# VectorE's program for a unit of experts: one text per class of size, odd and even together, weight pieces behind tests

## The chip, the cores and the metric

The kernel runs on one core of a Trainium2 chip. The metric is device time of one execution in microseconds; the time before is 594.67 us, the median of three runs (593.29 to 596.66). TensorE multiplies, ScalarE and VectorE work on tiles, GpSimd (POOL) gathers and scatters rows, and SyncE (SP) issues most DMAs. Each engine runs its own program and waits for the others on semaphores.

## The reference, cut to what matters

Attention over keys and values pooled by 8, then a mixture of 8 experts that sends each of the 4608 rows to one expert (top 1).

```python
k_p = k.reshape(B, H, Sp, 8, D).mean(axis=3)         # v likewise; B, H, S, D = 8, 8, 576, 64
attn = softmax(scale * q @ k_p.T); x = (attn @ v_p)  # -> x: 4608 rows of 512
expert_idx = np.argmax(x @ w_gate, axis=1)           # 8 experts
gate_w = softmax(x @ w_gate)[row, expert_idx]
for e in range(8):
    h = np.maximum(x[expert_idx == e] @ w1[e], 0.0)  # 512 -> 1024
    out[expert_idx == e] = gate_w * (h @ w2[e])      # 1024 -> 512
```

## The kernel before

**Stages.** The first 190 us or so are attention and routing: every row gets its expert and is scattered to a buffer in DRAM, sorted by expert. The rest is the expert stage, which the change concerns. There each expert's rows are cut into *units* of up to 512 rows (four blocks of 128). A unit's size is counted in halves of 64 rows, n from 1 to 8. How many units there are and how large is known only at run time: the kernel computes a table, every engine loads a unit's entries into registers and takes branches on them. The program text has 16 units one after the other, of which those above the number found are left out by a branch. With the inputs used there are 13, of sizes 8, 8, 1, 6, 4, 8, 5, 8, 4, 1, 8, 8, 6 (units 0 to 12); units 2, 3, 4, 5, 7, 9 and 10 open a new expert, so new weights come with them.

**One unit.** X (512 columns by rows) is split into a high and a low part for matmuls in fp32r; so are the weights W (eight pieces a expert, 0 to 3 of the first matrix, 4 to 7 of the second) and the hidden tiles H (eight, f = 0 to 7). ScalarE writes the high parts, VectorE the low ones: the high part is read back and subtracted (`hlo`, `hlo1` for H, `xlo` for X, `wlo` for W). TensorE multiplies X by W into H's banks, three of them in turn (`mm1`, its matmuls are line 890 in the trace): group f is 12 matmuls where n is above 2, and may start when the low part of the tile three before it, which used the same bank, is done; so a unit's fourth group waits for its first H part. Then it multiplies H by the second matrix (line 947) and VectorE scales the result by the gate into Y, block by block from the last; GpSimd scatters Y to the output.

**VectorE in a unit** (`dve_unit`), in the order of the text: (1) H's low parts (`hidden_lo`), with the low parts of weight pieces 4 to 7 between them where the unit is a new expert's, and behind H's sixth tile two transposes of the next unit's first two blocks (`xturn`); (2) the next unit's X (`following`, `next_part`, `xpart`): low parts of blocks 0 and 1, transposes of blocks 2 and 3, the last block of Y of the running unit (`early`), low parts of blocks 2 and 3, and among them weight pieces 0 to 3 if the next unit opens an expert; (3) two table loads and the rest of Y. An odd n takes three instructions for a Y block of one half, and two instead of one for each H tile.

**What sets the order.** It is written out by hand. A branch picks a text: `hidden_lo` has a text for n = 1, one for n = 2, one for even and one for odd n above 2 (lines 1238 and 1240); `following` has again a text for each of n = 1, above 2 and 2 (lines 1338 and 1343), and `next_part` in each of them one without and one with new weights (line 1268). A jump past a text is a branch of VectorE's own sequencer, which the profile does not count as busy.

## Time and profile before

| | |
|---|---|
| median of three runs | 594.67 us |
| profiled execution, whole | 594.27 us |
| its span, first to last instruction | 592.8 us |
| TensorE busy | 562.5 us (95%) |
| VectorE busy | 374.1 us (63%) |
| ScalarE busy | 241.2 us (41%) |
| GpSimd busy | 197.0 us (33%) |
| mean granted TensorE clock | 0.999 |

The span is the profiled execution's; 1.5 us of the run lie around it. A row of the timeline has the start, the duration (of all instructions merged in it), engine, line, operation, tiles out and in, the count, and in brackets the idle time of that engine before it with what ended it. "issue" there means that the engine waited for nothing that the profile shows. The names of banks in the trace are those of the attention stage, which the expert stage uses again: pP and pq are H's banks, pU is Y's, pS and pm are X's.

### The profile page before, as it was taken

The page shows a single profiled execution, that of the slowest core. Times are in us where ns is not written, and L with a number is a line of the kernel's source. Part 1 is how long each engine was busy: PE and PEld are TensorE (multiplying, and loading weights), DVE is VectorE, ACT ScalarE, POOL GpSimd, SP SyncE. Part 2 cuts the span into 40 slices and gives each one's busy share as a digit, 9 for nine tenths or more (in the row PEclk, how much of TensorE's full clock was granted, in tenths as well). Part 3 has the DMA queues.
Part 4 walks back from the last instruction along what each step waited for, and adds up shares of the span by engine and source line. Part 5 has one row for each costly group of instructions (what it writes and reads, how often), then busy time and mean ns, then how long its engine had stood idle before and what let it go on. Part 6 is the DMA issues. An engine that isn't in the chain of part 4 may idle for free.

```text
span 592.8 us, 13401 instructions
## 1 busy us (share of the span) xinstructions
PE 562.5 (95%) x4334; PEld 499.4 (84%) x4334; DVE 374.1 (63%) x738; ACT 241.2 (41%) x445; POOL 197.0 (33%) x294
## 2 busy tenths in 40 slices
PE   6889999999998999999997999989999999999995
PEld 5778989888887888879996888878899888888994
DVE  6699898888884224567968671684527967244221
ACT  2667686787631102355444420424115742021110
POOL 7456675655251032136222211122022442201101
PEclk9999999999999999999999999999999999999999
DMA  8979999896432647446995852027520860100101
GB/s 312 365 233 283 284 293 297 216 256 173 127 126 73 184 133 258 149 124 215 252 312 160 247 155 80 21 81 214 125 93 20 234 201 23 56 0 35 43 4 56
DMA packets 89019, 96.55 MB, mean 163 GB/s; under 512 B 38174, under 2 KB 69918, under 8 KB 88864
## 3 DMA queue, kind: packets, MB, share of 16 engines
q1 hardware_dynamic: 79472, 74.22, 43.5%
q0 software_dynamic: 8848, 20.55, 9.7%
q8 instruction: 60, 0.98, 0.8%
q14 instruction: 95, 0.78, 0.4%
q10 hardware_dynamic: 544, 0.02, 0.1%
HBM read 72.68 MB, written 26.00 MB: 166 GB/s over the span
## 4 chain that ended last, share of the span: by engine, by line
PE 69%; DVE 10%; issue 6%; POOL 5%; DMA 4%; ACT 3%; DVEq 1%; POOLq 1%; SPq 0%; ACTq 0%
PE pU L947 30%; PE pP L890 18%; PE pq L890 9%; PE pU L323 3%; POOL dispatched L432 2%; DMA XE<-in_v_dram 2%; PE pP L489 2%; DMA w<-in_moe_w_dram 2%; PE pP L307 1%; DVE mx L291 1%; PE pS L287 1%; POOL raw L196 1%; DVE sd L294 1%; DVE raw L196 1%; PE pq L489 1%
## 5 line engine op out<-in xcount | busy, mean ns | idle before, releaser
L947 PE MATMUL pU<-W,H 128*128 128x512 f32 x912 | 200.6, 380 | 4.0 <-DVE Y L1328 1.7
L947 PEld LDWEIGHTS pU<-W,H 128*128 128x128 f32 x912 | 171.5, 189 | 30.1 <-issue 2.5
L890 PE MATMUL pP<-X,W 128*128 128x512 f32 (+3 forms) x660 | 121.9, 340 | 5.8 <-DVE X L1157 3.6
L1545 POOL DMA_INDIRECT out_dram<-Y,GT x51 | 57.8, 1133 | 203.6 <-DVE Y L1330 168.7
L890 PEld LDWEIGHTS pP<-X,W 128*128 128x128 f32 x660 | 108.5, 190 | 15.8 <-DVE X L1157 4.0
L1082 ACT ACTIVATE H<-pP 128x512 fp32r<-128x512 f32 x56 | 33.5, 598 | 140.6 <-PE pP L890 134.2
L1330 DVE TENSOR_SCALAR Y<-pU,GT 128x512 f32<-128x512 f32 x36 | 26.6, 747 | 82.7 <-PE pU L947 81.7
L1103 DVE SCALAR_TENSOR_TENSOR H<-pP,H 128x512 fp32r<-128x512 f32 (+1 forms) x62 | 40.0, 645 | 53.5 <-ACT H L1082 51.4
L1183 ACT CAST W<-ST 128x1024 fp32r<-128x1024 f32 x56 | 56.8, 1051 | 27.5 <-PE pU L947 20.0
L1191 DVE TENSOR_TENSOR W<-ST,W 128x1024 fp32r<-128x1024 f32 x54 | 64.4, 1217 | 1.9 <-ACT W L1183 1.8
L890 PE MATMUL pq<-X,W 128*128 128x512 f32 (+3 forms) x324 | 62.5, 343 | 0.3 <-issue 0.3
L323 PE MATMUL pU<-V,pt 110*128 110x146 f32 (+3 forms) x468 | 56.7, 283 | 2.5 <-ACT pt L308 1.9
L890 PEld LDWEIGHTS pq<-X,W 128*128 128x128 f32 x324 | 53.7, 190 | 5.6 <-issue 0.8
L323 PEld LDWEIGHTS pU<-V,pt 110*128 110x128 f32 (+3 forms) x468 | 51.4, 179 | 4.2 <-ACT pt L308 2.9
L1552 POOL DMA_DIRECT2D GT<-dispatched x44 | 24.3, 552 | 82.9 <-issue 81.6
L432 POOL DMA_INDIRECT dispatched<-xe,ix x36 | 38.9, 1079 | 17.7 <-POOL ix L393 9.8
L1082 ACT ACTIVATE H<-pq 128x512 fp32r<-128x512 f32 x28 | 16.7, 597 | 60.8 <-PE pq L890 60.8
L1152 DVE STREAM_TRANSPOSE pS<-XE 128x512 f32<-128x512 f32 x26 | 37.9, 1499 | 0.0
L308 ACT COPY pt<-pP 110x384 f32<-110x384 f32 x72 | 30.8, 480 | 6.5 <-PE pP L307 5.8
L1103 DVE SCALAR_TENSOR_TENSOR H<-pq,H 128x512 fp32r<-128x512 f32 (+1 forms) x30 | 19.6, 655 | 21.2 <-ACT H L1082 20.6
L1143 ACT CAST X<-pS 128x512 fp32r<-128x512 f32 x34 | 19.2, 588 | 32.9 <-DVE pS L1152 22.6
L300 ACT ACTIVATE P<-sd 128x576 f32<-128x576 f32 x36 | 24.8, 689 | 19.0 <-DVE sd L294 17.1
(208 smaller groups left out, 651.8 us busy)
## 6 DMA issues: line engine op xcount, KB each, us to landing
ST<-in_moe_w_dram SPq DMA_DIRECT2D x56, 512.0 KB, 6.0
raw<-in_k_dram SPq DMA_DIRECT2D x12, 768.0 KB, 8.0
raw<-in_v_dram SPq DMA_DIRECT2D x11, 768.0 KB, 12.3
XE<-dispatched SPq DMA_DIRECT2D x104, 64.0 KB, 3.5
qa<-in_q_dram SPq DMA_DIRECT2D x24, 256.0 KB, 7.6
w<-in_moe_w_dram SPq DMA_DIRECT2D x8, 512.0 KB, 4.5
XE<-dispatched SPq DMA_DIRECT2D x15, 256.0 KB, 4.2
qa<-in_q_dram SPq DMA_DIRECT2D x2, 1024.0 KB, 11.3
```

Of the source, the lines that this page charges most:

```text
L308: take(out=pt[t][a][0:R], in_=pPs[a][0:R, 0 : 3 * P])
L323: nc.tensor.matmul(pu[p0 : p0 + n, a, h * VW : (h + m) * VW], lhsT=pt[t][a][0:r, c % 3 * P + p0 : c % 3 * P + p0 + n], rhs=Vs[g % 2][0:r, ...
L432: apart(nc.gpsimd.indirect_dma_start(out=xs, out_offset=bass.IndirectOffsetOnAxis(ap=at, axis=0), in_=rows, in_offset=None))
L890: r = pe.matmul(out=pH[g % 3][:, :m], lhsT=w1s(w, f, k), rhs=x, start=i == 0, stop=i == len(passes) - 1)
L947: r = pe.matmul(out=pY[:, s % 2, :], lhsT=h, rhs=in_turn(w[:, k * 512 : (k + 1) * 512]), start=start and i == 0, stop=stop and i == len(ps ...
L1082: act.activation(out=HH[:, f, o], in_=src[:, o], func=AF.Relu).then_inc(Q["A_h"], 1)
L1103: return dve.scalar_tensor_tensor(out=dst[:, f, to], in0=src[:, at], scalar=0.0, in1=f32(HH[:, f, at]), op0=ALU.max, op1=ALU.subtract)
L1152: dve.transpose(out=pX[:, s % 2, :].rearrange("p (c a g t) -> p c g t a", c=4, a=2, g=4), in_=XE[u % 2][:, s, :].rearrange("p (g r c) -> p ...
L1183: act.copy(out=(W1H if i < 4 else W2H)[:, o], in_=ST[:, i, :]).then_inc(Q["A_s1" if i < 4 else "A_s2"], 1)
L1191: eng.tensor_tensor(out=(W1L if i < 4 else W2L)[:, o], in0=ST[:, i, :], in1=f32((W1H if i < 4 else W2H)[:, o]), op=ALU.subtract).then_inc( ...
L1330: r = dve.tensor_scalar(out=rows(Y[:, s, :]), in0=a, scalar1=gate, scalar2=None, op0=ALU.mult)
L1545: pool.indirect_dma_start(out=out, out_offset=bass.IndirectOffsetOnAxis(ap=GT[:, u, s, 1:2].bitcast(I32), axis=0), in_=Y[:, s, :], in_offs ...
```

## The change

VectorE's program alone changes; the other engines' instructions stand in the same order. A unit's program is now chosen once by its class of size, n = 1, above 2, or 2, and each class has (1) and (2) in one text (`whole`). Odd and even n above 2 share one text, in which every H tile tests the parity (line 1109). The next unit's X has one text (`next_lo`), with tests around the weight pieces; of these, piece 1 now stands behind the X low parts of blocks 2 and 3 where it stood ahead of them. The order of the classes in the text is n = 1, above 2, 2; behind them stands (3) as before.

```diff
-            r = part(HL, o, o)
-            if odd is not None:
+            if odd is None:
+                part(HL, o, o).then_inc(Q["V_h"], 1)
+                return
+            with dve.If(odd == 0):
+                part(HL, o, o).then_inc(Q["V_h"], 1)
+            with dve.Else():
+                part(HL, o, o)
                 dve.drain()
-                r = part(HH, ds(odd + 64, 64), ds(odd, 64))
-            r.then_inc(Q["V_h"], 1)
+                at = 64 * nc.s_assert_within(entry(dve, K_U, u, 1, 8), 1, 7, ...) - 64
+                part(HH, ds(at + 64, 64), ds(at, 64)).then_inc(Q["V_h"], 1)
...
-        def hidden_lo(u, fs=range(8), small=True):
...
-                with dve.If(n % 2 == 0):
-                    go(8)
-                with dve.Else():
-                    go(7, 64 * ...)
...
+        def hidden_lo(u, n, fs=range(8)):
+            if n > 2:
+                odd = dve.snap(entry(dve, K_U, u, 1, 8) % 2, min_val=0, max_val=1)
+                turns = (lambda: more(dve, u + 1, lambda: [xturn(u + 1, s) for s in range(2)])) if u > 0 else lambda: None
+                return hidden(dve, u, lambda f: hlo(u, f, n, odd), wlo, lambda: vnop("V_s2", 4), fs, False, turns)
+            if n == 2:
+                return hidden(dve, u, lambda f: hlo(u, f, n), wlo, lambda: vnop("V_s2", 4), fs, True)
...
+        def next_lo(u, n, turn, mid=lambda: None):
+            new = entry(dve, K_SW, u, 0, 1) == 1
+            def pieces():
+                mid()
+                if n > 2:
+                    with dve.If(new):
+                        wlo(u, 0)
+            xpart(dve, u, lambda *a: xlo(*a, n <= 2), lambda v: xnone(u, v), pieces, turn)
+            with dve.If(new):
+                for i in range(1 if n != 2 else 0, 4):
+                    wlo(u, i, dve if n == 1 and i == 1 else None)
+            with dve.Else():
+                vnop("V_s1", 4)
...
-            def following():
-                go = lambda turn=None, small=False, **mid: next_part(dve, u + 1, ..., turn, between=0 if small else 2, **mid)
...
-            if u > 0:
-                hidden_lo(u)
-            more(dve, u + 1, following, alone)
+            def whole(size):
+                if size == 1:
+                    hidden_lo(u, 1)
+                    hlo1(u, 1)
+                    more(dve, u + 1, lambda: next_lo(u + 1, 1, None))
+                    return early()
+                hidden_lo(u, size)
+                more(dve, u + 1, lambda: next_lo(u + 1, size, early if size > 2 else None), early if size > 2 else lambda: None)
+                if size == 2:
+                    early()
+
+            if u == 0:
+                next_lo(1, 8, None, early)
+            else:
+                with dve.If(n < 2):
+                    whole(1)
+                with dve.Else():
+                    with dve.If(n > 2):
+                        whole(8)
+                    with dve.Else():
+                        whole(2)
```

**VectorE from unit 4's last H part to unit 5's weight pieces.** Line numbers after the change are five higher for X's parts and W's. Before, as it stands in the text for even n with new weights:

```order
L1103 SCALAR_TENSOR_TENSOR H<-pP_65,H 128x512
L1238 UNCONDITIONAL_BRANCH
...
L1338 COMPARE_AND_BRANCH
...
L1343 COMPARE_AND_BRANCH
L1268 COMPARE_AND_BRANCH
...
L1157 TENSOR_TENSOR X<-pS,X 128x8x64 x2
...
L1191 TENSOR_TENSOR W<-ST,W 128x1024 x2
L1132 COMPARE_AND_BRANCH
L1157 TENSOR_TENSOR X<-pS,X 128x8x64
```

and now:

```order
L1109 COMPARE_AND_BRANCH
L1103 SCALAR_TENSOR_TENSOR H<-pP_65,H 128x512
L1109 UNCONDITIONAL_BRANCH
...
L1162 TENSOR_TENSOR X<-pS,X 128x8x64 x2
L1124 COMPARE_AND_BRANCH
...
L1264 COMPARE_AND_BRANCH
L1196 TENSOR_TENSOR W<-ST,W 128x1024
L1264 UNCONDITIONAL_BRANCH
L1137 COMPARE_AND_BRANCH
L1162 TENSOR_TENSOR X<-pS,X 128x8x64
```

Before, the first dots leave out 75 rows, the second 53, the third 44, all jumped over; now only the odd variant's four rows lie between H and X, and one piece instead of two stands ahead of the second X parts.

**VectorE at the end of the one-half program of unit 2**, from the last weight pieces to the table loads that stand ahead of Y's last blocks. Before:

```order
L1191 TENSOR_TENSOR W<-ST,W 128x1024 x3
L1271 UNCONDITIONAL_BRANCH
L1358 COMPARE_AND_BRANCH
...
L824 COPY scr<-scr 128x1
L1370 UNCONDITIONAL_BRANCH
...
L771 TENSOR_LOAD tab
```

and now:

```order
L1196 TENSOR_TENSOR W<-ST,W 128x1024 x3
L1268 UNCONDITIONAL_BRANCH
...
L1342 COMPARE_AND_BRANCH
...
L824 COPY scr<-scr 128x1
L1354 UNCONDITIONAL_BRANCH
...
L771 TENSOR_LOAD tab
```

The instructions are the same, but from the last jump to the table load it is 148 rows of the text before and 198 now, since the hidden tiles of the two other classes stand behind this program where they stood ahead of it. At the end of the last unit, before the change, the jump past everything that belongs to a next unit is 198 rows long too.

## Rows read from the trace of the kernel before

**Rows 1.** The page: busy time by engine, and one instruction queue (packets, MB, share).
```profile
PE 562.5 (95%) x4334; PEld 499.4 (84%) x4334; DVE 374.1 (63%) x738; ACT 241.2 (41%) x445; POOL 197.0 (33%) x294
...
q14 instruction: 95, 0.78, 0.4%
```

**Rows 2.** TensorE's waits from 200 us on: us, times, longest; seven rows.
```profile
PE pP L890 <- DVE X L1157: 3.6, 1, 3.6
PE pU L947 <- DVE Y L1328: 1.7, 1, 1.7
...
PE pU L947 <- DVE H L1103: 0.8, 1, 0.8
...
PE pU L947 <- DVE W L1191: 0.2, 1, 0.2
```

**Rows 3.** Timeline of TensorE, unit 5's start: start, us, what, [idle before].
```profile
326.61 2.86 PE L890 MATMUL pP<-X,W 128*128 128x512 f32 x12 [3.64 <-DVE X L1157]
```

**Rows 4.** Timeline of VectorE, unit 4's end and unit 5's X.
```profile
316.04 0.68 DVE L1103 SCALAR_TENSOR_TENSOR H<-pP,H 128x512 fp32r<-128x512 f32 x1
318.95 1.29 DVE L1157 TENSOR_TENSOR X<-pS,X 128x512 fp32r<-128x512 f32 x2 [2.23 <-issue]
320.15 2.92 DVE L1152 STREAM_TRANSPOSE pS<-XE 128x512 f32<-128x512 f32 x2
...
323.03 2.33 DVE L1191 TENSOR_TENSOR W<-ST,W 128x1024 fp32r<-128x1024 f32 x2
325.28 1.28 DVE L1157 TENSOR_TENSOR X<-pS,X 128x512 fp32r<-128x512 f32 x2
```

**Rows 5.** Timeline of ScalarE, X's high part of block 1.
```profile
314.45 0.59 ACT L1143 CAST X<-pS 128x512 fp32r<-128x512 f32 x1 [0.83 <-DVE pS L1152]
```

**Rows 6.** Timeline of VectorE, unit 6's end and unit 7's X.
```profile
385.18 0.22 DVE L1103 SCALAR_TENSOR_TENSOR H<-pP,H  x1 [0.21 <-issue]
386.70 1.29 DVE L1157 TENSOR_TENSOR X<-pS,X 128x512 fp32r<-128x512 f32 x2 [1.29 <-issue]
```

**Rows 7.** Timeline of VectorE, first X part behind units 5 and 8.
```profile
349.18 1.29 DVE L1157 TENSOR_TENSOR X<-pS,X 128x512 fp32r<-128x512 f32 x2 [0.23 <-issue]
...
454.26 1.29 DVE L1157 TENSOR_TENSOR X<-pS,X 128x512 fp32r<-128x512 f32 x2 [1.08 <-issue]
```

**Rows 8.** Timeline of VectorE, last unit, behind its last H part.
```profile
575.25 0.16 DVE L824 COPY scr<-scr 128x1 f32<-128x1 f32 x1 [3.24 <-issue]
```

**Rows 9.** Timeline of SP's queue: weight loads.
```profile
269.36 9.95 SPq L1460 DMA_DIRECT2D ST<-in_moe_w_dram  x8
...
311.05 18.53 SPq L1460 DMA_DIRECT2D ST<-in_moe_w_dram  x8
...
394.39 5.10 SPq L1460 DMA_DIRECT2D ST<-in_moe_w_dram  x4
```

**Rows 10.** Timeline of VectorE inside unit 4's and unit 6's hidden tiles.
```profile
306.96 1.22 DVE L1191 TENSOR_TENSOR W<-ST,W 128x1024 fp32r<-128x1024 f32 x1
308.10 0.69 DVE L1103 SCALAR_TENSOR_TENSOR H<-pq,H 128x512 fp32r<-128x512 f32 x1
...
384.27 0.69 DVE L1103 SCALAR_TENSOR_TENSOR H<-pP,H 128x512 fp32r<-128x512 f32 x1 [0.39 <-issue]
```

**Rows 11.** Timeline of VectorE, end of units 2 and 9, next unit's first H.
```profile
272.40 0.69 DVE L1324 COPY Y<-pU 64x512 f32<-64x512 f32 x1 [0.59 <-issue]
...
274.48 0.67 DVE L1103 SCALAR_TENSOR_TENSOR H<-pP,H 128x512 fp32r<-128x512 f32 x1
...
476.42 0.15 DVE L824 COPY scr<-scr 128x1 f32<-128x1 f32 x1 [1.60 <-issue]
...
478.79 0.67 DVE L1103 SCALAR_TENSOR_TENSOR H<-pq,H 128x512 fp32r<-128x512 f32 x1
```

**Rows 12.** Timeline of TensorE, fourth groups of units 3 and 10.
```profile
275.47 4.13 PE L890 MATMUL pP<-X,W 128*128 128x384 f32 x24
...
479.77 2.75 PE L890 MATMUL pq<-X,W 128*128 128x512 f32 x12
```

## The prediction

> **What bounds the kernel now.** The page comes first: TensorE is busy 95% of the span [rows 1], so VectorE's edits count only where TensorE stands still for it. The list of TensorE's waits from 200 us on (all of the expert stage but its first unit) has seven rows that sum to 8.5 us, the longest 3.6 us and the last 0.2 us [rows 2]. That is all a faster VectorE could give back, 1.4% of the run; a VectorE that comes late can cost without such a limit.

> The 3.64 us stand ahead of unit 5 [rows 3]: TensorE is through with unit 4 at 326.61 - 3.64 = 322.97 and waits for the low parts of X of blocks 2 and 3. VectorE's rows show why they are late [rows 4]. It ends its last H low part at 316.72 and stands idle 2.23 us, put down to "issue", before the first X low part at 318.95, though ScalarE had the high part of that block ready at 314.45 + 0.59 = 315.04 [rows 5]. Then follow, without a gap, two X parts, two transposes (2.92), two weight pieces (2.33), and only then the two X parts that TensorE waits for. The 1.73 us in unit 6 have the same shape: 1.29 us idle by "issue", then X parts, transposes and the half block's three instructions on Y, for the last of which TensorE waits [rows 2, 6].

> What is the "issue" time? Between the last H low part and the first X part of a unit with more than two halves the old text takes jumps past the odd copy, the other sizes' program and, where the next unit opens an expert, the copy for a unit without new weights. Where that last jump is taken the idle time was 2.23, 1.29 and 1.08; where it isn't, 0.23 [rows 4, 6, 7]. The program itself comes by DMA: queue 14 brought 95 packets in 0.78 MB, 8.2 KB each [rows 1]. I read the idle time as VectorE waiting for a piece of program that it jumped to before it had come. The dearest such wait is the last unit's, 3.24 us, for a jump past some 198 rows of the order [rows 8]. The 2.23 us fell while eight weight loads were being issued (311.05 to 329.58), the 1.29 between loads, ahead of those from 394.39 on [rows 9], so loads may make such a wait 2.23 - 1.29 = 0.94 longer.

> **The change part by part.** *Large units.* One text instead of two, and X's part follows H's without a far jump. At the end of unit 4 the 2.23 us go, and one of the two weight pieces (2.33 / 2 = 1.17) moves behind the X parts that TensorE needs: 3.40 us earlier. What is late next: TensorE has 3.64 to win, so it still waits about 0.2, and I take 0.2 more for tests that now stand ahead of these parts: gain 3.2. The piece that moved is first needed with the third group of 12 matmuls, two groups of 2.86 us after the start [rows 3], so it is covered there; SP, which loads the next expert's piece once this one is split, gets it at 325.28 - 3.40 + 1.28 + 1.17 = 324.3 instead of 323.03 + 2.33 = 325.4, no later than now. Bounds: 1.2 (only the piece counts) and 3.64. At the end of unit 6 the 1.29 us go; that unit is odd and has two more tests with a taken jump behind the transposes, 0.2 each by the 0.21 and 0.39 us that stand ahead of its H parts today [rows 6, 10], so 0.9; some of it is lost to the first wait of 0.8 us, which these tests lengthen: gain 0.8, bounds -0.3 and 1.3. At the other boundaries TensorE does not wait for VectorE, and what VectorE saves there is worth nothing.

> *Tests per hidden tile.* Eight tests a large unit are added, and eight jumps past the odd text where the number is even. In unit 4, where VectorE is fullest, H parts and weight pieces follow each other without idle time today with a test between them (306.96 + 1.22, next at 308.10) [rows 10]: an instruction on data of 0.6 to 1.2 us covers the test behind it. Where VectorE waits for ScalarE the test now comes after the wait and delays that H part; the following three hidden tiles' slack covers it. Cost 0, bounds 0 and 0.2 a unit in the two units above, already counted.

> [...]

> *Units of one half* (2 and 9). Their program now stands first, and at its end VectorE jumps past both other programs, about 198 rows instead of 148, to reach the last Y parts. Behind that jump stand Y's three instructions and then the next unit's first H low part. Now there are 0.59 and 1.60 us of idle time there [rows 11]. The nearest row for 198 rows is the last unit's 3.24, the same distance. So 3.24 - 0.59 = 2.65 later in unit 2: the first H part of unit 3 starts at 274.48 + 2.65 = 277.13 and ends 0.67 later, at 277.80. TensorE's fourth group of unit 3 needs the bank that this part frees, and now starts at 275.47 [rows 12]: a new wait of 2.3. In unit 9: 3.24 - 1.60 = 1.64 later, the first H part ends at 478.79 + 1.64 + 0.67 = 481.10, and the fourth group of unit 10 now starts at 479.77: a new wait of 1.3. Eight weight loads start at 269.36, just as the first of these jumps is due [rows 9]; I add the 0.94 from above once. VectorE has room to catch up afterwards in units 3 and 10, so nothing more follows. Bounds: 0 (the jump costs what it costs today; coming earlier gives nothing, as TensorE does not wait there) and, for both together, 9.9: 2.3 + 1.3, twice 0.94, and twice 2.23 for the next jump right behind, past the program of one half at the start of units 3 and 10, should its piece not have come either.

> **Sum**, against the profiled execution: 594.27 - 3.2 - 0.8 + 2.3 + 1.3 + 0.9 = 594.8 us. That execution lies 0.4 under the median of the three shown (594.67), so I leave 594.8 as it is.

> **The rivals.** *The jump from the one-half program is cheap.* Then only the gains stay: 594.27 - 4.0 = 590.3. For it: today's jump of 148 rows there costs 0.59 in unit 2. Against it: the jump of equal length in the last unit cost 3.24, and nothing else was left for VectorE to do there.

> [...]

> *The one-half jump costs more than the gains: slower.* Its place is the turn from unit 2 to 3 and from 9 to 10, its price the full wait beside weight loads, 3.24 + 0.94 = 4.18 each, less what is paid today and the slack between the end of the first H part and TensorE's fourth group (0.59 + 275.47 - 275.15 and 1.60 + 479.77 - 479.46): 3.3 + 2.3 = 5.6, so 594.27 - 4.0 + 5.6 = 595.9; with a second missed jump at one of the places, 2.23 more, 598.1. It decides from a loss of 4.0 on, and is measurable from about 7.

> *The stall only moves.* If H and X of unit 4 fall into two pieces of program again, the 2.23 and 1.29 stay, the piece behind X gives 1.2, and the losses stay: 594.27 - 1.2 + 4.5 = 597.6. Against it: X's part now stands directly behind H's in the order, with no far jump between.

> **How the numbers follow.** Forecast 0.55, cheap jump 0.15, dear jump 0.18, moved stall 0.12. From no change the measurement can tell about 0.5%, 3.0 us: faster means under 591.7, slower over 597.6. The cheap jump gives faster in most of its cases, 0.13 in all with the forecast's lower edge; slower comes from the dear jump with a second miss and half of the moved stall, 0.14; the rest is 0.73. The likeliest case alone spans 593 to 596.5. The range 590.5 to 598.3 holds the cheap jump's time and the dear jump's upper one.

> **What would show it.** In the profile after: the idle time before the first X part of unit 5 falls from 2.23 to about 0.1, one weight piece stands ahead of the second pair of X parts and three behind, and TensorE's wait before unit 5 is under 0.6 us. The wait for Y in unit 6 is about 1 us. New are idle times by "issue" of about 3 us ahead of Y in units 2 and 9 and two TensorE waits for H inside the first matmuls of units 3 and 10, 2 to 3.5 and about 1.3 us. If those two waits are missing the time is near 590; if "issue" still stands before unit 5's X, the reading of the jumps is wrong.

## The result, and the profile after

The kernel after takes 600.03 us (median of seven runs, 597.19 to 602.61), the kernel before, beside it, 594.22 (592.14 to 596.66): a ratio of 1.0092, 95% interval 1.0066 to 1.0118. The change makes the kernel 0.9% slower. The forecast was 594.8 and its range ended at 598.3. The profiled execution took 602.61 us, 8.34 more than that of before; it is the slowest of the seven, 2.58 over their median, so its losses are the upper end of what the kernel shows.

To see where, I take the starts of each unit's first matmul group (line 890) from TensorE's timeline and subtract neighbours (units 1 and 2, and 8 and 9, together, since a unit of one half has other lines; the last from its first group to TensorE's end):

| us | 1+2 | 3 | 4 | 5 | 6 | 7 | 8+9 | 10 | 11 | 12 |
|---|---|---|---|---|---|---|---|---|---|---|
| before | 53.15 | 31.71 | 25.36 | 41.54 | 30.20 | 41.44 | 32.16 | 41.49 | 41.44 | 31.30 |
| after | 52.86 | 37.92 | 21.90 | 41.54 | 30.02 | 41.51 | 32.10 | 48.56 | 41.44 | 31.30 |

Unit 4 got 3.46 us shorter, units 3 and 10 got 6.21 and 7.07 longer, the other units together 0.46 shorter; unit 1 starts 0.84 earlier. The sum is 8.52 later at the end.

The page after, answering to [rows 1], with the granted clock in 40 slices:

```profile
PE 566.9 (94%) x4334; PEld 502.7 (84%) x4334; DVE 373.2 (62%) x738; ACT 241.1 (40%) x445; POOL 194.9 (32%) x294
...
PEclk9999999999999999998999999999999979999998
...
q14 instruction: 87, 0.71, 0.4%
```

TensorE has as many matmuls but is busy 4.4 us longer, and three slices show a granted clock under 9 tenths, where before had none: 270 to 285 us, 481 to 496 us, and the last, in which TensorE's work ends. TensorE's waits after (us, times, longest), answering to [rows 2]:

```profile
PE pP L890 <- DVE H L1103: 4.8, 1, 4.8
PE pq L890 <- DVE H L1103: 4.1, 1, 4.1
...
PE pU L947 <- DVE Y L1334: 0.3, 1, 0.3
```

The 3.64 and 1.73 of before are gone, or down to 0.3; in their place stand two waits for H. VectorE's timeline after, at the end of unit 4, against [rows 4]:

```profile
321.18 0.68 DVE L1103 SCALAR_TENSOR_TENSOR H<-pP,H 128x512 fp32r<-128x512 f32 x1
321.78 1.27 DVE L1162 TENSOR_TENSOR X<-pS,X 128x512 fp32r<-128x512 f32 x2
...
325.77 1.20 DVE L1196 TENSOR_TENSOR W<-ST,W 128x1024 fp32r<-128x1024 f32 x1
326.90 1.27 DVE L1162 TENSOR_TENSOR X<-pS,X 128x512 fp32r<-128x512 f32 x2
328.10 3.48 DVE L1196 TENSOR_TENSOR W<-ST,W 128x1024 fp32r<-128x1024 f32 x3
```

No idle time stands between H and X where 2.23 stood; one weight piece is ahead of the second X parts and three are behind. That is the change doing what it was read to do. The losses, on VectorE, at the turns from unit 2 to 3 and from 9 to 10, against [rows 11]:

```profile
274.60 0.15 DVE L824 COPY scr<-scr 128x1 f32<-128x1 f32 x1 [3.91 <-issue]
274.90 0.69 DVE L1330 COPY Y<-pU 64x512 f32<-64x512 f32 x1
...
278.30 0.15 DVE L824 COPY scr<-scr 128x1 f32<-128x1 f32 x1 [1.30 <-issue]
278.51 0.69 DVE L1103 SCALAR_TENSOR_TENSOR H<-pP,H 128x512 fp32r<-128x512 f32 x1
...
480.06 0.15 DVE L824 COPY scr<-scr 128x1 f32<-128x1 f32 x1 [3.73 <-issue]
...
484.52 0.15 DVE L824 COPY scr<-scr 128x1 f32<-128x1 f32 x1 [2.07 <-issue]
484.74 0.69 DVE L1103 SCALAR_TENSOR_TENSOR H<-pq,H 128x512 fp32r<-128x512 f32 x1
```

Each turn has two idle times by "issue": one behind the jump out of the one-half program, ahead of Y, and one behind the jump past the one-half program of the next unit, ahead of its first H part. TensorE's fourth groups, which wait for these H parts, against [rows 12]:

```profile
279.26 5.85 PE L890 MATMUL pP<-X,W 128*128 128x384 f32 x24 [4.75 <-DVE H L1103]
...
485.49 5.49 PE L890 MATMUL pq<-X,W 128*128 128x512 f32 x12 [4.08 <-DVE H L1103]
```

The waits are not all: the same 24 matmuls took 4.13 before and now 5.85, the same 12 took 2.75 and now 5.49. The busy times by stretch (the fields ahead of the last three are the engines' busy us; then granted clock, DMA share, GB/s) tell why. After:

```profile
274.00:279.00 5.00, 0.50 (x4) 0.20 (x2) 2.71 (x6) 3.33 (x5) 3.78 (x5) 1.00 0.99 342
279.00:286.00 7.00, 6.74 (x31) 6.75 (x32) 4.49 (x7) 2.13 (x3) 0.63 (x1) 0.76 1.09 288
480.00:485.00 5.00, 1.41 (x7) 0.90 (x5) 2.47 (x6) 3.18 (x5) 3.06 (x3) 0.92 0.77 237
485.00:492.00 7.00, 6.51 (x18) 5.29 (x19) 4.16 (x6) 0.98 (x2) 0.58 (x1) 0.57 0.46 102
```

and the second and fourth of these stretches before:

```profile
279.00:286.00 7.00, 7.00 (x44) 6.92 (x43) 5.40 (x7) 3.65 (x6) 2.09 (x2) 1.00 1.04 314
...
485.00:492.00 7.00, 7.00 (x34) 6.14 (x33) 5.45 (x6) 2.20 (x4) 2.21 (x4) 1.00 0.28 63
```

Right behind each gap the mean granted clock is 0.76 and 0.57 where it was 1.00 before: it is 0.50 from 279.36 to 282.77 us and from 484.2 to 490.9, and 1.00 behind both. In this execution unit 3 pays 4.75 of wait and 5.85 - 4.13 = 1.72 of clock, unit 10 pays 4.08 and 5.49 - 2.75 = 2.74.

### The profile page after: what moved, and what is told of

Its sections match the earlier page's. It is cut to its first block, busy times and chain, and to the rows that moved or that the text cites. A ratio compares the mean times of both kernels' runs of the same rounds, so it can differ in the third digit from the quotient of the medians.

```text
span 601.1 us, 13534 instructions
## 1 busy us (share of the span) xinstructions
PE 566.9 (94%) x4334; PEld 502.7 (84%) x4334; DVE 373.2 (62%) x738; ACT 241.1 (40%) x445; POOL 194.9 (32%) x294
## 4 chain that ended last, share of the span: by engine, by line
PE 66%; DVE 12%; issue 8%; POOL 5%; DMA 3%; DVEq 2%; ACT 2%; POOLq 1%; SPq 1%; ACTq 0%
PE pU L947 28%; PE pP L890 18%; PE pq L890 9%; PE pU L323 3%; POOL dispatched L432 2%; DMA XE<-in_v_dram 2%; DVE W L1196 2%; PE pP L489 2%; PE pP L307 1%; DVE mx L291 1%; POOL raw L196 1%; DVE raw L196 1%; PE pS L287 1%; DVE xe L339 1%; DVE sd L294 1%
## 5 line engine op out<-in xcount | busy, mean ns | idle before, releaser
L890 PE MATMUL pP<-X,W 128*128 128x512 f32 (+3 forms) x660 | 123.7, 344 | 6.7 <-DVE H L1103 4.8
L1548 POOL DMA_INDIRECT out_dram<-Y,GT x51 | 54.9, 1075 | 216.5 <-DVE Y L1336 181.8
L890 PEld LDWEIGHTS pP<-X,W 128*128 128x128 f32 x660 | 110.4, 192 | 17.0 <-DVE H L1103 5.0
L890 PE MATMUL pq<-X,W 128*128 128x512 f32 (+3 forms) x324 | 65.2, 353 | 4.8 <-DVE H L1103 4.1
L890 PEld LDWEIGHTS pq<-X,W 128*128 128x128 f32 x324 | 55.3, 195 | 11.2 <-DVE H L1103 4.5
L432 POOL DMA_INDIRECT dispatched<-xe,ix x36 | 39.9, 1109 | 18.4 <-POOL ix L393 9.8
L307 PE MATMUL pP<-ident,P 128*110 128x128 f32 x216 | 30.0, 275 | 0.6 <-ACT P L300 0.6
```

The source lines that it names most:

```text
L307: nc.tensor.transpose(pPs[a][0:R, c * P : (c + 1) * P], Ps[t % 2][:, o : o + R], ident)
L432: apart(nc.gpsimd.indirect_dma_start(out=xs, out_offset=bass.IndirectOffsetOnAxis(ap=at, axis=0), in_=rows, in_offset=None))
L890: r = pe.matmul(out=pH[g % 3][:, :m], lhsT=w1s(w, f, k), rhs=x, start=i == 0, stop=i == len(passes) - 1)
L1548: pool.indirect_dma_start(out=out, out_offset=bass.IndirectOffsetOnAxis(ap=GT[:, u, s, 1:2].bitcast(I32), axis=0), in_=Y[:, s, :], in_offs ...
```

## The experiments

**Theory.** A jump of VectorE's sequencer is dear where the piece of program it lands in has not come; the change made the jump out of the one-half program dear at both places and, with it, the next one; TensorE's gaps then lower its clock. **Rivals:** the merged text and its tests delay H; or the weight loads, not the gap, slow the matmuls.

**The jump alone (far).** On the kernel before, dead text in the program for n = 2, past which the one-half program jumps:

```diff
                         go(small=True)
                         early()
+                        for _ in range({2: 50, 9: 50}.get(u, 0)):
+                            dve.drain()
```

> The kernel before, with 50 instructions that never run put into the text that VectorE jumps past at the end of the one-half program of units 2 and 9; nothing that runs is changed. Theory (the length of that jump is the loss): VectorE stands idle 3.2 to 4 us by 'issue' ahead of Y's first instruction in both units where it stood 0.59 and 1.60, and TensorE gets two new waits for H with the fourth group of units 3 and 10, of about 3.0 and 1.8 us (3.9 - 0.59 and 3.7 - 1.60, less 0.3 of slack each), more if the next jump is late too; with up to 4 us for a lower clock behind them the time is 5 to 10 us above before. Rival (the merged text, its tests or the choice of class delay H in units 3 and 10, not the jump): no new waits, the time is that of before within 1.5 us.

Measured: 602.22 us, before 599.44 on the same chip, ratio 1.0034 (1.0001 to 1.0066). VectorE's rows of this run at the two places, then TensorE's:

```profile
276.72 0.15 DVE L824 COPY scr<-scr 128x1 f32<-128x1 f32 x1 [2.42 <-issue]
...
482.93 0.15 DVE L824 COPY scr<-scr 128x1 f32<-128x1 f32 x1 [2.62 <-issue]
```

```profile
279.84 4.17 PE L890 MATMUL pP<-X,W 128*128 128x384 f32 x24 [1.72 <-issue]
...
330.62 4.53 PE L890 MATMUL pP<-X,W 128*128 128x512 f32 x12 [3.67 <-DVE X L1157]
...
486.66 2.86 PE L890 MATMUL pq<-X,W 128*128 128x512 f32 x12 [1.28 <-DVE H L1103]
```

Instructions that never run make the two idle times 2.42 and 2.62 instead of 0.59 and 1.60 and give TensorE its two waits, at the fourth groups of units 3 and 10. So dead text in the jump's way is enough, without any test or merged text; it makes the jump longer and also moves all that follows, and this run does not tell the two apart. But it is a third of the loss: I expected 3.0 and 1.8 and 5 to 10 us in all. The second jump was not late in unit 3 and 0.52 in unit 10, the waits were short and the clock did not fall behind them (24 matmuls took 4.17, 12 took 2.86). It fell in unit 5 (0.79 from 326 to 334 us), behind the old wait for X of 3.67, where 12 matmuls took 4.53; behind 3.64 in [rows 3] they took 2.86.

**The order of the class texts (o812, o218).** On the kernel after, only which program stands where:

```diff
-                with dve.If(n < 2):
-                    whole(1)
+                with dve.If(n > 2):
+                    whole(8)
                 with dve.Else():
-                    with dve.If(n > 2):
-                        whole(8)
+                    with dve.If(n < 2):
+                        whole(1)
                     with dve.Else():
                         whole(2)
```

> The kernel after, with the order of the three class texts changed to above 2, 1, 2: the one-half program now jumps only past the program for n = 2. Theory (jump length): the idle times ahead of Y in units 2 and 9 fall from 3.9 and 3.7 to under 1.6 us, the TensorE waits of 4.75 and 4.08 us in units 3 and 10 go, and with them the lower clock behind them: 4.75 + 4.08 + 4.4 = 13 us less than after, 587 to 590; up to 594 if the jump into unit 9's program, now past the large text, is late in its place. Rival (the merged text and its tests make H late in units 3 and 10): the waits stay, 600.

Measured: 601.10, ratio 1.0034 (0.9997 to 1.0070). Units 3 and 10 take 31.69 and 41.44, as before the change, so the tests and the merged text cost them nothing, and that rival falls. But units 8 and 9 take 40.22 instead of 32.16: VectorE's entry into unit 9's program, and TensorE for it, in this run:

```profile
466.27 2.36 DVE L1196 TENSOR_TENSOR W<-ST,W 128x1024 fp32r<-128x1024 f32 x2 [7.00 <-issue]
```

```profile
472.39 5.24 PE L947 MATMUL pU<-W,H 128*128 128x512 f32 x16 [7.29 <-issue]
```

The dear jump moved from the end of the one-half program to its start, at nearly twice the price, and the 16 matmuls behind the gap took 5.24 instead of 3.69. For a late entry I had allowed up to 594, no more than before; the ratio came out above that at its middle, though its interval reaches 0.9997. Unit 2's entry, some 141 rows by my count, was not dear (0.39 of idle time ahead of its first weight piece); unit 9's is some 170. The other order (2, 1, above 2):

> The kernel after, with the order of the class texts changed to 2, 1, above 2: the one-half program jumps past the large text alone, the large one falls through to Y. Theory (length alone decides): about 147 and 175 rows, like before, so the waits in units 3 and 10 go both, 587 to 592. A finer theory (VectorE's program comes in pieces of the 8.2 KB packets, and it is late where a jump leaves out a whole piece): by counting rows the jump of unit 2 reaches the next piece and that of unit 9 leaves one out, so only unit 3's wait goes and unit 10's stays at 3 to 4 us with its lower clock: 593 to 596. Rival (merged text and tests): both waits stay, 600.

Measured: 598.75, ratio 0.9973 (0.9943 to 1.0002). Unit 3's wait for its first H part is gone (it takes 32.62 us; a wait of 0.77 at its sixth group is left), unit 10 still takes 46.57, by rows of VectorE and of TensorE in this run:

```profile
276.30 0.15 DVE L824 COPY scr<-scr 128x1 f32<-128x1 f32 x1 [0.30 <-issue]
...
478.04 0.15 DVE L824 COPY scr<-scr 128x1 f32<-128x1 f32 x1 [3.00 <-issue]
```

```profile
483.37 4.49 PE L890 MATMUL pq<-X,W 128*128 128x512 f32 x12 [3.18 <-DVE H L1103]
```

The same jump past the same text costs 0.30 in unit 2 and 3.00 in unit 9, as the finer theory had it and the bare length did not (the two are about 147 and 175 rows, though, so length with a sharp edge is not excluded by this run alone).

The traces agree with pieces that come late in one thing: a packet of 8192 bytes lands in every dear jump at the end of a one-half program, and the first table load starts 1.1 to 1.5 us later ("What the idle times are made of", below). How many rows of the program such a packet holds no run shows, so the length of the piece that I counted with, here and in the versions that place unit 9, was not shown.

**Where the pieces fall (best2).** The run above, with dead instructions ahead of unit 9 in texts that no unit here runs (n = 2):

```diff
                     whole(2)
+                    for _ in range({4: 9, 5: 9, 6: 8, 7: 8, 8: 8}.get(u, 0)):
+                        dve.drain()
```

> The run with class order 2, 1, above 2, with 42 instructions that never run added in the texts for n = 2 of units 4 to 8 (9, 9, 8, 8, 8), so that everything from unit 9 on stands 42 rows further in VectorE's program; no jump there gets shorter and nothing that runs is changed. Finer theory (a jump is dear where it leaves out a whole piece of program, and by counting rows unit 9's exit now reaches the next piece): the idle time ahead of Y in unit 9 falls from 3.00 to under 1.5 us, that ahead of unit 10's first H part from 1.95 to under 1, TensorE's wait of 3.2 us in unit 10 shrinks under 1 and unit 10 takes 41.5 to 43.5 us instead of 46.57; the whole is 3 to 5 us under that run, 0.5 to 1% under before. Rival (the length of the jump alone decides): unit 10 stays at 46 to 47 us.

Measured: 596.33 against 593.81, ratio 1.0040 (1.0017 to 1.0062). A half hit. VectorE in units 9 and 10:

```profile
472.64 0.15 DVE L824 COPY scr<-scr 128x1 f32<-128x1 f32 x1 [0.54 <-issue]
...
475.10 0.15 DVE L824 COPY scr<-scr 128x1 f32<-128x1 f32 x1
480.75 0.69 DVE L1103 SCALAR_TENSOR_TENSOR H<-pq,H 128x512 fp32r<-128x512 f32 x1 [5.51 <-issue]
```

With the jump's length unchanged its price fell from 3.00 to 0.54 (0.56 in both runs of best3 below, where unit 9 stands some 50 rows further): place decides, not length. But 5.51 stand ahead of unit 10's first H part, and it takes 47.49. The COPY at 475.10 is the first instruction of unit 10's large program, so the jump into it came through at once; the wait stands behind it, where no jump is taken. I take it that the jump landed a few rows ahead of the border of a piece, and that my count was off by these few; where the borders lie no run shows.

**The clock (warm, warm2).** The kernel after, with TensorE busy in the gaps:

```diff
+                if f == 3:
+                    for _ in range({(3, 6): 26, (10, 8): 22}.get((u, n), 0)):
+                        pe.matmul(out=pD[:, 0:128], lhsT=ident, rhs=ident, start=True, stop=True)
                 if g >= 3:
                     pe.wait_ge(Q["V_h"], g - 2)
```

> The kernel after, with matmuls whose result nobody reads put ahead of TensorE's wait for H in the fourth groups of units 3 and 10 (26 and 22 of 128 columns, some 4.1 and 3.5 us), so that TensorE works in most of the two gaps. Theory (the gaps lower the granted clock, which was 0.76 and 0.57 right behind them, and this is 4.4 of the loss): the 24 matmuls of 5.85 us and the 12 of 5.49 behind the waits take 4.13 and 2.75 again, VectorE's idle times stay, the time is about 4.4 us under after, 595.6. Rival (the weight loads make these matmuls slow, whatever TensorE did before): they stay at 5.5 to 5.9 us and the time is that of after, 600, or some tenths above.

Measured: 604.53, ratio 1.0077 (1.0047 to 1.0106). The matmuls behind took 4.15 and 2.84 and the clock of the run was 0.998, as expected; the ratio lies among those of the kernel after on other chips (1.0057 to 1.0143), so no gain of the whole time is shown. The added matmuls were dearer than I counted (5.97 and 5.07 us) and ended 0.2 us behind H in unit 3 and 3.3 in unit 10, where H came early in this run. So I made them fewer (22 and 12):

> The kernel after, with fewer of the matmuls whose result nobody reads (22 and 12 instead of 26 and 22) ahead of the wait for H in units 3 and 10, so that they end before H comes. Theory (the gap lowers the clock): the 24 matmuls behind them take 4.1 to 4.2 us instead of 5.85 in unit 3, the 12 of unit 10 2.8 to 4.5 instead of 5.49, and units 3 and 10 get shorter by about that, 1.7 and 1 to 2.6 us, at equal lateness of H. Rival (lateness of H is all, the clock costs nothing): both units last as long as in after.

Measured, in a single run: 598.74 us. TensorE in unit 3, and in unit 10:

```profile
275.23 5.07 PE L887 MATMUL pm<-ident 128*128 128x128 f32 x44
280.27 4.17 PE L893 MATMUL pP<-X,W 128*128 128x384 f32 x24
...
484.04 2.86 PE L893 MATMUL pq<-X,W 128*128 128x512 f32 x12 [1.35 <-DVE H L1106]
```

At the same lateness of H (VectorE's idle times in unit 2 were 3.94 and 1.25) the 24 matmuls take 4.17 and unit 3 takes 36.37 instead of 37.92, with the weight loads as they were; the granted clock was 1.00 from 280 to 287 us, where the profile after had 0.76 from 279 to 286. The gap, not the loads, lowers the clock in unit 3. Unit 10 takes 45.81 instead of 48.56.

**The kernel after again (ctrl, ctrl_b).** On two more chips:

> The kernel after again, beside the others on one chip: 1.0% above before on the same chip (0.6 to 1.3), with unit 3 some 6 us and unit 10 some 5 to 7 us longer than before (31.71 and 41.49) and unit 4 some 3.4 us shorter. Every theory expects this; it gives the others their comparison.

> The kernel after beside it: ratio 1.006 to 1.015 to before, units 3 and 10 longer by 6 to 8 and 2 to 7 us. Both theories expect this.

Measured: ratios 1.0143 (1.0096 to 1.0190) and 1.0057 (1.0033 to 1.0082). Units 3 and 10 took 39.35 and 43.27, then 38.47 and 42.89. In the first of these runs:

```profile
279.58 6.86 PE L890 MATMUL pP<-X,W 128*128 128x384 f32 x24 [5.18 <-DVE H L1103]
...
483.23 2.86 PE L890 MATMUL pq<-X,W 128*128 128x512 f32 x12 [1.57 <-DVE H L1103]
```

Unit 3's loss is there each time, unit 10's second jump is sometimes late (2.07 in the profile after) and sometimes not (0.23 in this run): 1.57 of wait, and no lower clock behind it (2.86 for the 12 matmuls). So unit 10 lost 1.8 and 1.4 here, less than I had expected (5 to 7, then 2 to 7), and units 3 and 10 together 9.42 and 8.16 where the profile after has 13.28.

**The piece behind X alone (piece, piece5).** On the kernel before, one number:

```diff
-                                                                     between=0 if small else 2, **mid)
+                                                                     between=0 if small else 1, **mid)
```

> The kernel before, with one edit: in large units the second weight piece of the next expert stands behind the X low parts of blocks 2 and 3. Theory of the prediction (2.23 us of idle time and 1.17 us of this piece make the 3.64 us wait): TensorE's wait ahead of unit 5 falls by 1.2 to 2.5 and unit 4 lasts 24.2 instead of 25.36; units 3, 6 and 10 stay. Rival (the wait is the idle time alone, the piece beside it is hidden): the wait stays at 3.6.

> The kernel before with the second weight piece behind X alone, timed: unit 4 took 22.84 us instead of 25.36 in one look. If that holds the time is 1.2 to 2.5 us under before, ratio 0.996 to 0.998; if unit 10's longer time of that look (43.21) belongs to the edit it is 0.998 to 1.001.

Measured: 593.15 in a single run; timed 597.28 against 599.16, ratio 0.9988 (0.9958 to 1.0018), so not to be told from no change. The wait ahead of unit 5 fell from 3.64 to 1.2 and 1.4, unit 4 to 22.84 and 23.16. Only 1.17 of that is the piece; in the first of these profiles the idle time before X was also shorter:

```profile
316.51 1.29 DVE L1157 TENSOR_TENSOR X<-pS,X 128x512 fp32r<-128x512 f32 x2 [0.85 <-issue]
```

0.85 where [rows 4] had 2.23: the price of one and the same jump varies by more than a microsecond between executions. Unit 10's 43.21 of the single run did not come again (41.52): in it the jump out of unit 9, which the edit does not touch, left 3.14 of idle time ahead of Y, where it left 1.60 before and 1.26 in the timed run, and TensorE waited 1.42.

**A version without the dear jumps (best3, best3b).** The kernel after, with the large program first in the two units behind a one-half unit, so that they start without a jump, and 50 dead instructions that place unit 9:

```diff
+                if u in (3, 10):
+                    with dve.If(n > 2):
+                        whole(8)
...
+                else:
+                    with dve.If(n == 2):
+                        whole(2)
+                        for _ in range({4: 10, 5: 10, 6: 10, 7: 10, 8: 10}.get(u, 0)):
+                            dve.drain()
...
```

> The kernel after, with the class order above 2, 1, 2 in units 3 and 10 (the units behind those of one half, which then start without a jump) and 2, 1, above 2 in all others, and 10 instructions that never run in the texts for n = 2 of units 4 to 8. Finer theory (a jump is dear only where it leaves out a whole piece of program): by counting rows no jump next to the one-half units leaves one out, so ahead of Y in units 2 and 9 and ahead of the first H part of units 3 and 10 VectorE is idle under 1 us, TensorE has no wait above 1 us in units 3 and 10, they take 31.7 and 41.5 us as before the change, unit 4 takes 21.9 instead of 25.36 and unit 6 29.0 to 29.5 instead of 30.2; the whole is 4 to 5 us under before, ratio 0.991 to 0.994. Rival (the merged text itself delays H): units 3 and 10 stay 4 to 7 us longer.

> The version without a dear jump next to the one-half units again, on one chip with the kernel after. Theory (the jumps and the clock behind them are all that the change lost): units 3 and 10 take 31.7 and 41.5 to 42.3 us, the ratio to before is 0.988 to 0.996, 1.2 to 2% under after. Rival (the gain of the first timing, 0.9907, belongs to that chip's slow runs of before): the ratio is 0.997 to 1.002.

Measured: 593.38 against 599.16, ratio 0.9907 (0.9878 to 0.9936); on another chip 588.87 against 595.42, ratio 0.9897 (0.9860 to 0.9933), where the kernel after had 1.0057. It beats both. VectorE's rows at the two turns of the second run:

```profile
269.42 0.15 DVE L824 COPY scr<-scr 128x1 f32<-128x1 f32 x1 [0.33 <-issue]
...
469.33 0.15 DVE L824 COPY scr<-scr 128x1 f32<-128x1 f32 x1 [0.56 <-issue]
```

No idle time stands ahead of the first H parts of units 3 and 10. Unit 10 takes 41.52, unit 4 21.99, unit 6 29.02; in the first run unit 10 took 42.27, with 2.59 of idle time by "issue" behind its first H part. Unit 3 takes 33.34 and not 31.7: a wait of TensorE at the start of unit 4, put down to "issue" (1.62 us in the first run, 1.44 in the second), which the kernel with the piece alone had on the first run's chip too (1.28); I did not follow it. The placement is tuned to the sizes of these inputs, so it shows the cause and is no general cure.

**What the idle times are made of.** The views above leave out the instructions of VectorE's sequencer and single packets of queue 14; the kept traces have both. At the end of the one-half program the last test ahead of the jump (line 1370 before, 1354 after) and the first table load behind it start this far apart:

| us | before | after | far | o218 | best2 | best3, best3b |
|---|---|---|---|---|---|---|
| unit 2 | 0.49 | 4.09 | 2.76 | 0.49 | 0.49 | 0.49 |
| unit 9 | 0.95 | 3.69 | 2.76 | 2.93 | 0.51 | 0.50 |

With both exits of ctrl, ctrl_b, warm and warm2 there are 13 gaps above 2.7 us, up to 4.86. In each of the 13 a packet of 8192 bytes of queue 14 lands, and the first table load starts 1.1 to 1.5 us after its end; in best2 the wait ahead of unit 10's first H part ends 1.56 after such a landing. The trace does not say which engine a packet is for, and with 75 of them in the last 400 us a landing alone would prove little; the nearly constant time from landing to load is my ground for reading the gap as VectorE waiting for a piece of its program.

The price in the timeline is another number than this gap. The weight pieces still running hide its first 2 us or so; and the two table loads with the tests behind them, 1.84 us, ran beside weight pieces before and stand bare where the gap is long. So the 3.91 of the profile after is 2.07 without an instruction and 1.84 of loads and tests, and far's 2.42 is 0.57 and 1.85.

## Why the prediction was wrong

The sum said 594.27 + 0.5; the profiled execution came to + 8.34. Step by step:

- **Unit 4 to 5, gain 3.2: right.** Unit 4 is 3.46 shorter; the idle time is gone, one piece ahead and three behind, as written. But the list of idle times at such turns left one out: unit 3 is followed by a new expert too and takes the same jumps, and its last H part (288.42, 0.70 us long) and the first X part (289.02) had no idle time between them. The price did not go by the jump taken there either.
- **Unit 6 to 7, gain 0.8: right in kind.** 0.18 in the profiled run, where unit 6 ended on another wait of 0.76; 1.1 to 1.3 in the two later profiles of the same kernel (29.10 and 28.93 instead of 30.20).
- **Tests per hidden tile, 0: right.** Units 5, 7, 11 and 12 last as long to within 0.07 us, and with another order of the texts units 3 and 10 do too.
- **One-half units, + 2.3, + 1.3 and 0.9 for loads: the place and the engine right, the size wrong.** This is the step that failed. Waits of 4.5 in all were forecast; 4.75 + 4.08 = 8.83 came. The jump out of the one-half program was nearly right: 3.91 and 3.73, or 7.64, where the sum had twice 3.24 and 0.9, or 7.4. That is luck in part: the price was taken from a jump of equal length, but o218 and best2 show that the length does not set it, and the 1.84 of table loads and tests in each of the two are not in the last unit's 3.24, behind which the loads come later. The second jump, past the next unit's one-half program, was late at both places, 1.30 and 2.07, or 3.37 of the 4.33 missing. I had it in the bound (9.9) and in a rival with one such miss (598.1), and left it out of the sum. Between the two idle times of a turn VectorE had only Y's three instructions and some table loads, 2.40 us in all at the first turn and 2.39 at the second, so there was little to cover a second late jump once the first had been late. Some 0.7 is spread over small rows.
- **The clock: not in the sum, nor in a rival, nor in the bound.** 1.72 + 2.74 = 4.46 us in the profiled execution, over half of its miss; in ctrl, where only unit 3's clock fell, the 24 matmuls alone took 6.86 - 4.13 = 2.73 longer. The prediction priced a late H by TensorE's wait alone. The 3.64 us wait of before had left the clock at 1.00 (326.6 to 330 us), but one row was no ground to take the clock for free: the runs have a fall behind waits of 3.18, 3.67, 4.03 and more, and none behind 1.2 to 1.7.

So the waits were 4.33 too small, the clock 4.46, the gains 0.36 too large; 0.84 came back ahead of unit 1 and 0.29 in units 1 and 2. Together that is 8.0, against the 7.8 between 8.34 and 0.5; small differences of the other units make up the rest. This is the account of the slowest of seven executions; the median lies 5.2 above the sum. The "dear jump" rival had the right mechanism and the right price for one place; the forecast had 0.55 for a smaller one. The "cheap jump" and the stall that "only moves" are refuted by the rows above. The range was to hold the cheap jump's time, but its lower end, 590.5, lies above that time, 590.3.

What stays open: why the gap of a dear jump runs from 2.8 to 4.9 us at the end of the one-half program and to 7 at unit 9's entry in o812, and differs by a microsecond or more between executions of one program. Several of these fall beside weight loads, but no run took the loads away, since units 3 and 10 wait for those weights.

## What to carry to other kernels

Where an engine's program seems to come in pieces while it runs, as the landings ahead of 13 late table loads suggest here, the order of alternatives is part of the schedule: look where each taken jump lands next to a wait that another engine feels, and count the jumps behind it too, since one late jump can be followed by another (1.30 and 2.07 us here, though 0.23 in another execution). Here the order of the texts and some text that never runs moved the ratio between 1.0057 and 0.9897 on one chip, so a change that "only" reorders or shortens code should be read with the order of both programs, place by place. A late producer cost TensorE its wait here and, behind most waits of 3.18 us and more, a lower clock (12 matmuls in 4.49 to 5.49 us instead of 2.75 to 2.86); price both. And an idle time by "issue" is not all one wait: table loads and tests that a late jump leaves bare are in it, 1.84 of the 3.91 us in the profile after.
